# Attention, soft mixture of experts and a feed-forward layer: V's shifted copy made by GpSimd, larger expert transfers, first tokens loaded for two pairs

## The chip, the cores and the metric

The kernel runs on one core of a Trainium2 chip. The metric is device microseconds per execution; the kernel before took 448.73 us (median of three runs, 447.17 to 449.23). One further execution was profiled; it took 445.32 us, and the profile covers 443.6 us of it. Five engines matter: TensorE (PE), VectorE (DVE), ScalarE (ACT), GpSimd (POOL) and SyncE (SP), whose queue issues nearly all DMAs.

## What is computed

```python
# q, k, v: (4 batches, 8 heads, 576 tokens, 64), float32
scores = q @ k.T / 8 + slope[h] * -(i - j)      # only 0 <= i - j < 128, else -1e9
attn_out = softmax(scores) @ v                  # then (2304, 512)
logits = x @ phi                                # 32 slots: 8 experts x 4
slot_input = softmax(logits, over tokens).T @ x
slot_out[e] = relu(slot_input[e] @ w1[e]) @ w2[e]     # w1 (8,512,1024), w2 (8,1024,512)
x = softmax(logits, over slots) @ slot_out
out = leaky_relu(x @ w_in, 0.01) @ w_out        # w_in (512,2048), w_out (2048,512), float64
```

The expert weights are 33.5 MB, `w_in` and `w_out` 16.8 MB, and q, k and v 14.2 MB together.

## The kernel before

The program has three stages. The attention stage handles the 32 (batch, head) combinations as 16 pairs of heads. While it runs, the expert weights are loaded beside it into every free piece of SBUF. The expert stage then multiplies the 32 slots by the weights (`L772`, `L824`), and the feed-forward stage does the rest (`L925`, `L948`).

**A pair's work.** `load_qk` brings the tokens 64 to 575 of k and of q (256 KB each, `put` at `L185`) and the tokens 0 to 63 (32 KB each, `L186`). `relay` (RK, RQ) lets GpSimd reorder k and q in SBUF (`L255`), `turn` (TK, TQ) and `turn_rest` (TR) transpose them on PE (`L262`, `L268`), and `evac_k`, `evac_q`, `evac_rest` (EK, EQ, ER) copy the results out of PSUM. `scores` (SX, SY) multiplies (`L297`), `smax` (M) adds the mask and takes the maximum on DVE (`L314`), `expo` (E) takes the exponential on ACT (`L325`), `flip` (F) transposes (`L336`) and `flip_c` (C) copies back. `attend` (AV, `L368`) multiplies by V, `sums` and `norm` (NS, NO) divide, `turn_x` (TX, `L398`) transposes the result for the logits.

**V in two layouts.** The windows of 128 keys start at multiples of 64. `E` (`ve`) holds V with token 128 t + p on partition p, `O` (`vo`) the same shifted by 64 tokens. Both have two buffers. `load_v` loads `E` with one transfer for each head, and the last 64 tokens of `O` with a third. The other parts of `O` are copied from `E` between the two halves of the partitions by two transfers within SBUF (`L194`, `L195`):

```python
put(O[64:128, 0:4], E[0:64, 0:4], n + DVO, ("v", i))     # 130 KB
put(O[0:64, 1:4], E[64:128, 0:3], n + DVO, ("v", i))     # 97.5 KB
```

**What sets the order.** Each step of pair i stands at 2 i + `XO[step]` on one axis; the steps of the batches use `YO`. All steps are sorted by this number, and each engine gets its instructions in that order. `put` notes a transfer with its place on the axis; `issue`, called at three points in every unit, has SP issue the transfers whose place has passed (`send`, `L156`), and then as many weight pieces of 256 KB (`L171`) as a credit of `L0` (later `L1`) per unit allows. A pair takes two units of the axis. SP works through its queue strictly in order: a transfer that must wait for a buffer or for data holds back all behind it. The program also gives the DMAs eight completion counters in turn, and a DMA on one of them is issued after the DMA eight places earlier has landed.

**Weight pieces.** 71 pieces of 256 KB fit beside the attention (14 slots of 4 pieces, `qx`, `ex`, `frx`, `ql`). 26 more go into buffers that the last pairs leave, among them `nat` (6 pieces), where k and q arrive. The last 31 pieces follow in transfers of 1 MB (`L789`) as the expert stage empties the slots.

Of the kernel before, what the change touches and what calls it, by code (L numbers as in the profile page):

```python
# [18 lines left out]
def attn_softmoe_ffn(ctx: ExitStack, tc: tile.TileContext, q, k, v, phi, w1, w2, w_in, w_out, cst_in, out):  # L19
    nc = tc.nc  # L20
    B, H, S, D = q.shape
    NT, DM = out.shape
    NS = phi.shape[1]
# [11 lines left out]
    NQ, NL = 3, 8  # L35
    HI = 3
    WN = [5, 2, 0, 2, 3, 0, 0]
    XO = {"RK": -5.833, "RQ": -4.884, "TR": -4.438, "TK": -4.435, "EK": -4.019, "ER": -3.744, "TQ": -3.472, "EQ": -3.389,
# [4 lines left out]
    YO = {"lg": 4.307, "lga": 4.375, "lh": 8.258, "lgc": 8.43, "lx": 8.469, "pm": 9.118, "ln": 9.618, "bm": 9.798,  # L43
          "bmv": 10.183, "bmx": 10.399, "lnc": 10.502, "bt": 10.836, "btv": 10.874, "dxv": 10.922, "tm2": 11.205,
          "dxa": 11.366, "sl": 11.714, "bta": 11.761, "slv": 11.994, "tm3": 12.06, "tme": 12.179, "cb": 12.909,
          "cb2": 12.964, "cb3": 13.232, "ds": 13.281, "dsv": 13.416, "cb4": 14.733}
    LAST = {"li": 6.35, "lgi": 6.568}
    ZA = {"DQK": 0.8, "DV": 0.3, "DVS": 0.3, "DVO": 1.4, "W0": -2.2, "EARLY": 0.8, "L0": 2.85, "L1": 3.6, "I1": 0.7769, "I2": 0.7995, "I3": 0.86}
    DQK, DV, DVS, DVO, W0, EARLY = [ZA[x] for x in ("DQK", "DV", "DVS", "DVO", "W0", "EARLY")]
    XI = [ZA[x] % 1 for x in ("I1", "I2", "I3")]  # L50
    NEG = -1.0e30
    SLOT = 2048
# [55 lines left out]
    def put_w(i, j0, t):  # L108
        n = t.shape[1] // 512
        for j in range(n):  # L110
            W[units_w[i]][j0 + j] = t[:, 512 * j:512 * j + 512]
        return t.rearrange("p (e f) -> p e f", e=n), src_w(i, j0, j0 + n)

    with tc.manual_schedule():
# [43 lines left out]
        def put(o, i, n, key):  # L158
            bulk.insert(sum(x[2] <= n for x in bulk), (o, i, n, key))
# [17 lines left out]
        natx = [view("nat", 512, 2048 + 512 * half) for half in range(2)]  # L177

        def natr(i):
            return view("nat", 128, 3072 + 128 * (i % 2))  # L180

        def load_qk(half, i, n=-9):
            b, h = divmod(2 * i, H)
            src, t = (k, q)[half][b, h:h + 2], nat(half, i)
            put(t.rearrange("p (h c) -> p h c", h=2), src[:, 64:S, :].rearrange("h (p t) d -> p h (t d)", t=4), n, (half, i))  # L185
# [11 lines left out]
        for half in (1, 0):  # L197
            load_qk(half, 0)
        for j in range(2):
            o, i, _, _ = bulk.pop(2 - j)  # L200
# [20 lines left out]
        for half in (1, 0):  # L221
# [4 lines left out]
        load_v(1)  # L226
        issue(1)
# [7 lines left out]
        pieces += [(NG - 2 + max(XO[nm] for nm in ("TK", "TQ", "TR")) + .001, view("nat", 512, 512 * j)) for j in range(6)]  # L235

        def queue(r, t, at=None):
            i, j = divmod(nxt_piece[0] if at is None else at, 4)
            nxt_piece[0] += at is None
            low.append((r, *put_w(i, j, t)))  # L240
        nxt_piece = [0]
        late = len(pieces) + (off["x0"] - off["x2"]) // 512 + 13
        for r, t in pieces[:-6]:
            queue(r, t)
        for j in range(NL):
            queue(W0, ql[:, 512 * j:512 * j + 512], late + j)
# [126 lines left out]

# [33 lines left out]
        def batch_parts(b):  # L407
# [160 lines left out]
            def dsv():  # L568
# [3 lines left out]
                else:  # L572
# [509 lines left out]
```

## Time and profile before

| | |
|---|---|
| median of three runs | 448.73 us |
| profiled execution, its span | 445.32 us, 443.6 us |
| PE / DVE / ACT / POOL busy | 406.3 / 241.5 / 221.8 / 40.2 us |
| attention: first to last `attend` | 22.47 to 170.00 us |
| expert stage: first `L772` | 181.42 us |
| HBM read / written | 64.75 MB / 4.72 MB |

Times count from the start of the span. A busy PE is not a PE at its peak; in the attention stage the granted clock of TensorE changes from stretch to stretch, and an `attend` of 68 matmuls takes 1.99 us or up to 3.4 us. An engine's idle time is put down to what ended it. SP's rows (SPq) are the times that its queue spent on issuing.

### The profile page before, as it was taken

What the parts mean: (1) busy time and instruction counts of PE and PEld (TensorE: products, weight loads), DVE (VectorE), ACT (ScalarE), POOL (GpSimd) and SP (SyncE); (2) the same over time, 40 slices, a digit from 0 to 9 for tenths busy, and PEclk for the clock granted to TensorE, in tenths of its full rate; (3) what the DMA queues carried; (4) which work ended last, traced back from release to release, by engine and by line L of the source; (5) the groups of instructions that cost most, each with busy time, mean ns of one, the idle gap of its engine ahead of it and who ended that gap; (6) DMA issues with size and microseconds to landing.
All of it is one profiled execution on the core that took longest, in us unless ns stands there. A gap on an engine that the chain in (4) does not pass through costs nothing.

```text
span 443.6 us, 10375 instructions
## 1 busy us (share of the span) xinstructions
PE 406.3 (92%) x4012; PEld 326.6 (74%) x4012; DVE 241.5 (54%) x824; ACT 221.8 (50%) x546; POOL 40.2 (9%) x71
## 2 busy tenths in 40 slices
PE   6997779786778995999999999999999999999996
PEld 6896668586767884433777788878878888888885
DVE  2675648375658584303599867686572223225242
ACT  2765637364647471111696765555555335333330
POOL 3111111111111101202000002020202000000000
PEclk9998969898989899999999999999999999999999
DMA  5697888897998769999996203100000003003011
GB/s 154 155 290 225 256 243 235 245 264 224 258 254 253 217 159 332 350 388 392 407 396 243 95 1 118 73 0 1 1 0 1 0 0 143 1 0 144 0 72 71
DMA packets 63137, 73.88 MB, mean 167 GB/s; under 512 B 27760, under 2 KB 37360, under 8 KB 63088
## 3 DMA queue, kind: packets, MB, share of 16 engines
q1 hardware_dynamic: 62528, 72.79, 51.9%
q8 instruction: 32, 0.52, 0.5%
q10 hardware_dynamic: 560, 0.43, 0.3%
q14 instruction: 17, 0.14, 0.1%
HBM read 64.75 MB, written 4.72 MB: 157 GB/s over the span
## 4 chain that ended last, share of the span: by engine, by line
PE 75%; DMA 17%; SPq 2%; DVE 2%; issue 1%; POOL 0%; ACT 0%; ACTq 0%; DVEq 0%; POOLq 0%
PE acc L948 45%; DMA ar<-ar 8%; PE g L368 7%; DMA ar<-in_v_dram 6%; PE ph L925 4%; PE pb L772 3%; PE pb L824 3%; PE g L336 2%; PE g L262 2%; PE g L297 2%; DVE ss L314 1%; SPq L171 1%; DMA p<-in_moe_w_dram 1%; PE g L150 1%; SPq L156 1%
## 5 line engine op out<-in xcount | busy, mean ns | idle before, releaser
L948 PE MATMUL acc<-p,p 128*128 128x512 f32 x648 | 158.8, 390 | 0.0
L948 PEld LDWEIGHTS acc<-p,p 128*128 128x128 f32 x648 | 120.7, 188 | 24.6 <-issue 1.7
L938 DVE TENSOR_TENSOR p<-ar,p 128x384 fp32r<-128x384 f32 x96 | 53.0, 555 | 92.1 <-ACT ar L934 91.9
L930 ACT ACTIVATE p<-ph 128x384 fp32r<-128x384 f32 (+1 forms) x97 | 47.5, 491 | 93.1 <-PE ph L925 93.1
L368 PE MATMUL g<-ar,pt 64*64 64x65 f32 (+1 forms) x1088 | 40.1, 253 | 26.4 <-DMA ar<-ar 22.4
L368 PEld LDWEIGHTS g<-ar,pt 64*64 64x64 f32 (+1 forms) x1088 | 36.2, 162 | 30.9 <-issue 15.2
L325 ACT ACTIVATE ss<-ss,mx 128x192 f32<-128x192 f32 x144 | 51.5, 431 | 14.3 <-DVE mx L314 14.3
L948 PE MATMUL acc<-b,p 128*128 128x512 f32 x216 | 54.4, 395 | 0.0
L934 ACT ACTIVATE ar<-ph 128x384 f32<-128x384 f32 x96 | 47.0, 489 | 0.0
L948 PEld LDWEIGHTS acc<-b,p 128*128 128x128 f32 x216 | 40.1, 188 | 8.8 <-issue 0.2
L314 DVE CUSTOM_DVE_ANT_0 ss<-g,ar 128x192 f32<-128x192 f32 x128 | 38.2, 354 | 11.4 <-PE g L303 6.4
L925 PE MATMUL ph<-p,p 128*128 128x384 f32 x96 | 33.0, 349 | 0.0
L255 POOL COPY ar<-ar 128x512 f32<-128x512 f32 x32 | 19.6, 616 | 125.8 <-DMA ar<-in_k_dram 84.5
L297 PE MATMUL g<-kqt 64*64 64x192 f32 (+2 forms) x768 | 27.5, 281 | 0.0
L378 DVE TENSOR_SCALAR rs<-g 128x4 f32<-128x4 f32 x32 | 3.7, 157 | 42.5 <-PE g L368 42.5
L297 PEld LDWEIGHTS g<-kqt 64*64 64x64 f32 x768 | 24.5, 135 | 3.1 <-issue 1.8
L277 ACT ACTIVATE kqt<-g,qsc 128x512 f32<-128x512 f32 x16 | 11.0, 688 | 29.9 <-PE g L262 29.7
L336 PE MATMUL g<-ident,ss 128*128 128x128 f32 x208 | 25.9, 275 | 0.0
L718 DVE SCALAR_TENSOR_TENSOR ar<-ar 128x512 int32<-128x512 int32 x40 | 25.6, 684 | 0.2
L336 PEld LDWEIGHTS g<-ident,ss 128*128 128x128 f32 x208 | 23.8, 144 | 0.2 <-issue 0.2
L718 POOL TENSOR_TENSOR p<-ar,p 128x512 fp32r<-128x512 f32 x8 | 10.8, 1348 | 125.6 <-ACT p L718 109.0
L262 PE MATMUL g<-ident,ar 128*128 128x128 f32 x128 | 21.9, 298 | 0.0
(191 smaller groups left out, 458.4 us busy)
## 6 DMA issues: line engine op xcount, KB each, us to landing
p<-in_moe_w_dram SPq DMA_DIRECT2D x56, 256.0 KB, 4.2
p<-in_moe_w_dram SPq DMA_DIRECT2D x7, 1024.0 KB, 11.4
p<-in_moe_w_in_dram SPq DMA_DIRECT2D x5, 1024.0 KB, 9.0
p<-in_moe_w_out_dram SPq DMA_DIRECT2D x5, 1024.0 KB, 14.1
out_dram<-ar SPq DMA_DIRECT2D x17, 256.0 KB, 2.1
ar<-in_q_dram SPq DMA_DIRECT2D x16, 256.0 KB, 4.6
ar<-in_v_dram SPq DMA_DIRECT2D x32, 128.0 KB, 3.9
ar<-in_moe_w_dram SPq DMA_DIRECT2D x16, 256.0 KB, 5.3
```

The costliest lines, as they stand in the source:

```text
L262: nc.tensor.transpose(p[:, bass.ds(t, 128, step=4)], natx[half][:, 128 * t:128 * t + 128], ident)
L297: nc.tensor.matmul(sts[i, a, c][64 * u:64 * u + 64, o:o + n], lhsT=Q[r, 64 * e:64 * e + 64], rhs=K[r, 64 * e - 64 + k:64 * e - 64 + k + n] ...
L314: nc.vector.tensor_tensor_reduce(out=e[:, w], in0=p[:, w], in1=maskt[:, m:m + 192], op0=ALU.add, op1=ALU.min, accum_out=mx[i % 2][:, n:n + ...
L325: nc.scalar.activation(out=e[:, w], in_=e[:, w], func=AF.Exp, scale=-1.0, bias=mx[i % 2][:, n:n + 1])
L336: nc.tensor.transpose(p[:, 128 * j:128 * j + 128], x, ident)
L368: nc.tensor.matmul(o[n][64 * u:64 * u + 64, W * x:W * x + W], lhsT=P, rhs=V, start=bool(st), stop=bool(sp), tile_position=(r, 64 * u))
L718: l.append(lambda: f(*a, **kw))
L925: nc.tensor.matmul(p, lhsT=mst[:, 128 * f:128 * f + 128], rhs=rhs, start=True, stop=True)
L930: nc.scalar.activation(out=G[t0, f][0][:, c], in_=H1[t0, f][:, c], func=AF.Prelu, alpha=0.01)
L934: nc.scalar.activation(out=gg, in_=H1.pop((t0, f)), func=AF.Prelu, alpha=0.01)
L938: nc.vector.tensor_tensor(out=g2, in0=G0.pop((t0, f)), in1=g1.bitcast(F32), op=ALU.subtract)
L948: nc.tensor.matmul(acc[t0][t], lhsT=(g1, g1, g2)[k][:, 128 * t:128 * t + 128], rhs=(WO1, WO2, WO1)[k][c][:, i], start=(f == f0 and k == 0) ...
```

## The change

`load_v` no longer issues the two transfers within SBUF. A new step VS (`shift_v`) makes the same two copies with GpSimd instructions; it stands at 2 i - 2.49, ahead of AV at 2 i - 1.213. The 14 slots and later pieces are cut so that a slot is loaded by two transfers of 512 KB where four of 256 KB were used; a transfer of 512 KB takes two credits. The tokens 0 to 63 of k and q are loaded by `load_r` for two pairs at a time (64 KB each), so `nat` grows by 256 columns and `ex` shrinks by as many: 70 pieces fit beside the attention, and `nat` later takes 7. The numbers of `XO`, `YO`, `LAST` and `ZA` are new throughout; the transfers of k and q are now placed after both relays of the pair, the weights begin at -5.5 instead of -2.2, and `L0` is 2.55 instead of 2.85.

```diff
-    XO = {"RK": -5.833, "RQ": -4.884, "TR": -4.438, "TK": -4.435, "EK": -4.019, "ER": -3.744, "TQ": -3.472, "EQ": -3.389,
+    XO = {"RQ": -6.287, "TR": -5.772, "RK": -5.368, "ER": -5.24, "TQ": -4.686, "TK": -4.445, "EK": -4.038, "EQ": -3.861,
...
-    ZA = {"DQK": 0.8, "DV": 0.3, "DVS": 0.3, "DVO": 1.4, "W0": -2.2, "EARLY": 0.8, "L0": 2.85, "L1": 3.6, "I1": 0.7769, "I2": 0.7995, "I3": 0.86}
+    ZA = {"DQK": 0.05, "DV": 0.3, "DVS": 0.3, "W0": -5.5, "EARLY": 0.8, "L0": 2.55, "L1": 3.6, "I1": 0.7769, "I2": 0.7995, "I3": 0.86}
...
-                r, o, i = low.pop(0)
+                r, w, o, i = low.pop(0)
                 nc.sync.dma_start(out=o, in_=i)
-                credit[0] -= 1
+                credit[0] -= w
...
-            return view("nat", 128, 3072 + 128 * (i % 2))
+            return view("nat", 128, 3072 + 128 * (i % 4))
...
-            put(natr(i)[64 * half:64 * half + 64].rearrange("p (h d) -> p h d", h=2), src[:, 0:64, :].rearrange("h p d -> p h d"), n, (2, i))
+        def load_r(half, i, n=-9):
+            b, h = divmod(2 * i, H)
+            put(view("nat", 256, 3072 + 128 * (i % 4))[64 * half:64 * half + 64].rearrange("p (h d) -> p h d", h=4), (k, q)[half][b, h:h + 4, 0:64, :].rearrange("h p d -> p h d"), n, (2, i))
...
-            E, O = [w[i % NVB].rearrange("p t h d -> p t (h d)") for w in (ve, vo)]
-            put(O[64:128, 0:4], E[0:64, 0:4], n + DVO, ("v", i))
-            put(O[0:64, 1:4], E[64:128, 0:3], n + DVO, ("v", i))
...
-            pieces += [(W0, t[:, 512 * j:512 * j + 512]) for j in range(4)]
+            pieces += [(W0, t[:, 1024 * j:1024 * j + 1024]) for j in range(2)]
...
-                    load_qk(half, i + 2, 2 * i + XO["TR"] + DQK)
+                    load_qk(half, i + 2, 2 * i + max(XO[nm] for nm in ("TR", "RK", "RQ")) + DQK)
+                if i % 2 and i + 3 < NI:
+                    load_r(half, i + 3, 2 * i + XO["TR"] + DQK)
...
+        def shift_v(i):
+            flush(("v", i))
+            E, O = [w[i % NVB].rearrange("p t h d -> p t (h d)") for w in (ve, vo)]
+            nc.gpsimd.tensor_copy(O[64:128, 0:4], E[0:64, 0:4])
+            nc.gpsimd.tensor_copy(O[0:64, 1:4], E[64:128, 0:3])
```

SP's queue in a round of the middle of the attention, before: k, q and V of a later pair (`L156`), weight pieces (`L171`), the two transfers within SBUF (`ar<-ar`), and more pieces.

```order
L156 DMA ar<-in_k_dram 128x2x256
L156 DMA ar<-in_k_dram 64x2x64
L156 DMA ar<-in_q_dram 128x2x256
L156 DMA ar<-in_q_dram 64x2x64
L156 DMA ar<-in_v_dram 128x4x64 x2
L156 DMA ar<-in_v_dram 64x2x64
L171 DMA p_157<-in_moe_w_dram 128x512 x2
L171 DMA p_158<-in_moe_w_dram 128x512
L156 DMA ar<-ar 64x520
L156 DMA ar<-ar 64x390
L171 DMA p_158<-in_moe_w_dram 128x512 x3
```

Two rounds of the same part now, with the first tokens (64x4x64) in one of the two:

```order
L156 DMA ar<-in_k_dram 64x4x64
L156 DMA ar<-in_q_dram 64x4x64
L156 DMA ar<-in_k_dram 128x2x256
L156 DMA ar<-in_q_dram 128x2x256
L171 DMA p_154<-in_moe_w_dram 128x2x512
L156 DMA ar<-in_v_dram 128x4x64 x2
L156 DMA ar<-in_v_dram 64x2x64
L171 DMA p_155<-in_moe_w_dram 128x2x512
L156 DMA ar<-in_k_dram 128x2x256
L156 DMA ar<-in_q_dram 128x2x256
L171 DMA p_155<-in_moe_w_dram 128x2x512
```

A round had 15 transfers, 6 of them weight pieces. Now three transfers of V and one weight transfer follow the last row shown, and two rounds have 17 transfers: 2 of first tokens, 4 of k and q, 6 of V, and 5 of weights (10 pieces).

GpSimd's queue before, from its first relay on (`L255`; `L448` belongs to the logits):

```order
L255 COPY ar<-ar 128x512 x15
L448 TENSOR_TENSOR ar<-bm_102,ar 128x64
L255 COPY ar<-ar 128x512 x8
L448 TENSOR_TENSOR ar<-bm_102,ar 128x64
L255 COPY ar<-ar 128x512 x8
```

And now (the relay is `L257`, the copies of V are `L378` and `L379`):

```order
L257 COPY ar<-ar 128x512 x4
L378 COPY ar<-ar 64x520
L379 COPY ar<-ar 64x390
L257 COPY ar<-ar 128x512 x2
L378 COPY ar<-ar 64x520
L379 COPY ar<-ar 64x390
L257 COPY ar<-ar 128x512 x2
```

Each pair of relays now has the two copies of V of an earlier pair ahead of it, and those wait for that V to land.

PE's order around an `attend` also changed. Before, the transposes of k and q stood at its two sides and the flips (`L336`) followed in one block:

```order
L303 MATMUL g<-kqt 64x64 x2
L297 MATMUL g<-kqt 64x192 x4
L297 MATMUL g<-kqt 64x128 x4
L297 MATMUL g<-kqt 64x64 x4
L268 MATMUL g<-ident,ar 128x128
L262 MATMUL g<-ident,ar 128x128 x4
L368 MATMUL g<-ar,pt_93 64x65 x2
```

Now `attend` (`L371`) follows the scores (`L301`) at once, and the transposes (`L264`) come between the flips (`L340`) behind it:

```order
L301 MATMUL g<-kqt 64x192 x4
L301 MATMUL g<-kqt 64x128 x4
L301 MATMUL g<-kqt 64x64 x4
L371 MATMUL g<-ar,pt_93 64x65 x2
L371 MATMUL g<-ar,pt_95 64x65 x2
```

## Rows read from the trace of the kernel before

**Rows 1.** Stretches: PE, PEld, DVE, ACT, POOL busy; PE clock; DMA share; GB/s.
```profile
0.00:22.40 22.40, 18.47 (x194) 16.86 (x194) 10.19 (x58) 10.60 (x29) 4.80 (x14) 1.00 0.62 155
22.40:170.00 147.60, 120.52 (x2352) 107.66 (x2351) 93.10 (x480) 84.48 (x231) 17.26 (x30) 0.92 0.85 241
170.00:181.40 11.40, 9.18 (x142) 6.93 (x142) 5.59 (x24) 2.00 (x10) 4.17 (x11) 1.00 1.03 369
181.40:216.50 35.10, 34.83 (x313) 12.83 (x314) 8.26 (x33) 6.86 (x16) 3.22 (x8) 1.00 1.02 378
```

**Rows 2.** Chain that ended last, in order of time: start, us, what.
```profile
94.88 4.92 DMA ar<-in_v_dram
99.85 3.35 DMA ar<-ar
103.33 3.40 PE g L368 x68
```

**Rows 3.** Waits from 22.4 to 170 us: total us, times, longest (PE, then SP).
```profile
PE g L368 <- DMA ar<-ar: 19.1, 8, 3.3
...
SPq L156 <- DMA ar<-in_v_dram: 12.6, 11, 1.7
```

**Rows 4.** Timeline of SP's queue, one round: start, us, instructions.
```profile
81.83 1.13 SPq L156 DMA_DIRECT2D ar<-in_k_dram  x2
83.05 1.25 SPq L156 DMA_DIRECT2D ar<-in_q_dram  x2
84.39 1.75 SPq L156 DMA_DIRECT2D ar<-in_v_dram  x3
86.20 1.86 SPq L171 DMA_DIRECT2D p<-in_moe_w_dram  x3
88.83 1.15 SPq L156 DMA_DIRECT2D ar<-ar  x2
90.01 1.56 SPq L171 DMA_DIRECT2D p<-in_moe_w_dram  x3
...
91.67 1.14 SPq L156 DMA_DIRECT2D ar<-in_k_dram  x2
```

**Rows 5.** SP's issues of 1 MB: count, ns min/median/max, first and last start.
```profile
L789 SPq DMA_DIRECT2D p<-in_moe_w_dram x8: 367/438/4072, 182.5 to 195.5; - x8
```

**Rows 6.** Five rounds, scores to scores (columns as rows 1); first and sum.
```profile
26.94:33.71 6.77, 6.77 (x149) 6.21 (x148) 5.80 (x31) 5.65 (x16) 0.60 (x2) 1.00 0.96 285
...
sum 36.47, PE 35.16 PEld 32.31 DVE 31.23 ACT 27.97 POOL 0.87; mean PE 7.03 PEld 6.46 DVE 6.25 ACT 5.59 POOL 0.17
```

**Rows 7.** DMA issues: operation, count, KB each, median us to landing.
```profile
p<-in_moe_w_dram SPq DMA_DIRECT2D x56, 256.0 KB, 4.2
p<-in_moe_w_dram SPq DMA_DIRECT2D x7, 1024.0 KB, 11.4
...
ar<-in_v_dram SPq DMA_DIRECT2D x32, 128.0 KB, 3.9
...
ar<-ar SPq DMA_DIRECT2D x16, 130.0 KB, 3.2
```

**Rows 8.** One stretch of 10 us with DMA nearly full (columns as rows 1).
```profile
110.00:120.00 10.00, 7.40 (x152) 6.82 (x152) 6.48 (x36) 5.79 (x17) 1.08 (x2) 1.00 0.92 268
```

**Rows 9.** GpSimd's instructions on the arena: count, ns min/median/max, span, form.
```profile
L255 POOL COPY ar<-ar x32: 611/616/619, 4.9 to 150.2; 128x512 f32<-128x512 f32 x32
L718 POOL TENSOR_TENSOR p<-ar,p x8: 1307/1314/1590, 273.6 to 337.7; 128x512 fp32r<-128x512 f32 x8
```

**Rows 10.** PE's timeline at the first and last `attend`: start, us, instructions, idle before.
```profile
20.10 0.71 PE L150 MATMUL g<-ident 128*128 128x128 f32 x4
...
22.47 0.75 PE L368 MATMUL g<-ar,pt 128*64 128x65 f32 x18
...
170.00 1.99 PE L368 MATMUL g<-ar,pt 128*64 128x65 f32 x68 [3.25 <-DMA ar<-ar]
...
181.42 2.78 PE L772 MATMUL pb<-p,ar 128*32 128x512 f32 x24 [0.36 <-ACT ar L620]
```

More of the change, by code (lines that the diff above doesn't have):

```diff
@@ L37, in attn_softmoe_ffn @@
     WN = [5, 2, 0, 2, 3, 0, 0]
-    XO = {"RK": -5.833, "RQ": -4.884, "TR": -4.438, "TK": -4.435, "EK": -4.019, "ER": -3.744, "TQ": -3.472, "EQ": -3.389,
[4 rows of a table removed]
[L43 to L47, printed above, removed]
-    ZA = {"DQK": 0.8, "DV": 0.3, "DVS": 0.3, "DVO": 1.4, "W0": -2.2, "EARLY": 0.8, "L0": 2.85, "L1": 3.6, "I1": 0.7769, "I2": 0.7995, "I3": 0.86}
-    DQK, DV, DVS, DVO, W0, EARLY = [ZA[x] for x in ("DQK", "DV", "DVS", "DVO", "W0", "EARLY")]
+    XO = {"RQ": -6.287, "TR": -5.772, "RK": -5.368, "ER": -5.24, "TQ": -4.686, "TK": -4.445, "EK": -4.038, "EQ": -3.861,
[4 rows of a table added]
+    YO = {"lg": 3.21, "lga": 3.902, "lh": 6.995, "lgc": 7.809, "lx": 8.264, "pm": 8.326, "ln": 8.841, "bm": 9.098,
+          "lnc": 9.721, "bmv": 9.864, "tm2": 10.117, "bmx": 10.288, "dxv": 10.428, "tm3": 10.497, "bt": 10.674,
+          "btv": 10.881, "dxa": 10.989, "sl": 11.047, "tme": 11.471, "bta": 11.518, "slv": 11.756, "ds": 11.96,
+          "dsv": 12.03, "cb": 12.432, "cb2": 12.523, "cb3": 12.626, "cb4": 13.203}
+    LAST = {"li": 5.561, "lgi": 5.608}
+    ZA = {"DQK": 0.05, "DV": 0.3, "DVS": 0.3, "W0": -5.5, "EARLY": 0.8, "L0": 2.55, "L1": 3.6, "I1": 0.7769, "I2": 0.7995, "I3": 0.86}
+    DQK, DV, DVS, W0, EARLY = [ZA[x] for x in ("DQK", "DV", "DVS", "W0", "EARLY")]
     XI = [ZA[x] % 1 for x in ("I1", "I2", "I3")]
@@ L72, in attn_softmoe_ffn @@
     XG = 5 * 4 * D
-    sizes = [("nat", 3328), ("ex", 8512 - 3328 - XG - NVB * VW), ("x2", XG), ("vt0", VW), ("vt1", VW), ("x0", XG), ("x1", XG),
+    sizes = [("nat", 3584), ("ex", 8512 - 3584 - XG - NVB * VW), ("x2", XG), ("vt0", VW), ("vt1", VW), ("x0", XG), ("x1", XG),
              ("maskt", 384), ("xT", 1152), ("L", 336)]
@@ L179, in natr @@
         def natr(i):
-            return view("nat", 128, 3072 + 128 * (i % 2))
+            return view("nat", 128, 3072 + 128 * (i % 4))
         def load_qk(half, i, n=-9):
             b, h = divmod(2 * i, H)
-            src, t = (k, q)[half][b, h:h + 2], nat(half, i)
-            put(t.rearrange("p (h c) -> p h c", h=2), src[:, 64:S, :].rearrange("h (p t) d -> p h (t d)", t=4), n, (half, i))
-            put(natr(i)[64 * half:64 * half + 64].rearrange("p (h d) -> p h d", h=2), src[:, 0:64, :].rearrange("h p d -> p h d"), n, (2, i))
+            put(nat(half, i).rearrange("p (h c) -> p h c", h=2), (k, q)[half][b, h:h + 2, 64:S, :].rearrange("h (p t) d -> p h (t d)", t=4), n, (half, i))
+        def load_r(half, i, n=-9):
+            b, h = divmod(2 * i, H)
+            put(view("nat", 256, 3072 + 128 * (i % 4))[64 * half:64 * half + 64].rearrange("p (h d) -> p h d", h=4), (k, q)[half][b, h:h + 4, 0:64, :].rearrange("h p d -> p h d"), n, (2, i))
         def load_v(i, n=-9):
@@ L192, in load_v @@
             put(vo[i % NVB][64:128, 4, :, 0:D], v[b, h:h + VH, 512:S, :].rearrange("h p d -> p h d"), n + DVS, ("v", i))
-            E, O = [w[i % NVB].rearrange("p t h d -> p t (h d)") for w in (ve, vo)]
-            put(O[64:128, 0:4], E[0:64, 0:4], n + DVO, ("v", i))
-            put(O[0:64, 1:4], E[64:128, 0:3], n + DVO, ("v", i))
-        for half in (1, 0):
-            load_qk(half, 0)
+        for f in (load_qk, load_r):
+            for half in range(2):
+                f(half, 0)
         for j in range(2):
-            o, i, _, _ = bulk.pop(2 - j)
+            o, i, _, _ = bulk.pop(0)
             nc.scalar.dma_start(out=o, in_=i)
@@ L220, in attn_softmoe_ffn @@
         nc.vector.memset(ones, 1.0)
-        for half in (1, 0):
+        for half in range(2):
             load_qk(half, 1)
@@ L226, in attn_softmoe_ffn @@
         load_v(1)
+        for half in range(2):
+            load_r(half, 2)
         issue(1)
@@ L234, in attn_softmoe_ffn @@
         pieces += [(W0, frx)]
-        pieces += [(NG - 2 + max(XO[nm] for nm in ("TK", "TQ", "TR")) + .001, view("nat", 512, 512 * j)) for j in range(6)]
+        pieces += [(NG - 2 + max(XO[nm] for nm in ("TK", "TQ", "TR")) + .001, view("nat", 512, 512 * j)) for j in range(7)]
         def queue(r, t, at=None):
             i, j = divmod(nxt_piece[0] if at is None else at, 4)
-            nxt_piece[0] += at is None
-            low.append((r, *put_w(i, j, t)))
+            nxt_piece[0] += t.shape[1] // 512 if at is None else 0
+            low.append((r, t.shape[1] // 512, *put_w(i, j, t)))
         nxt_piece = [0]
-        late = len(pieces) + (off["x0"] - off["x2"]) // 512 + 13
-        for r, t in pieces[:-6]:
+        late = sum(t.shape[1] // 512 for _, t in pieces) + (off["x0"] - off["x2"]) // 512 + 13
+        for r, t in pieces[:-7]:
             queue(r, t)
@@ L246, in attn_softmoe_ffn @@
             queue(W0, ql[:, 512 * j:512 * j + 512], late + j)
-        for r, t in pieces[-6:]:
+        for r, t in pieces[-7:]:
             queue(r, t)
@@ L265, in turn_rest @@
         def turn_rest(i):
-            flush((2, i))
+            flush((2, i - i % 2))
             tps[2, i] = p = gt((128, 128))
@@ L347, in attend @@
         def attend(i):
-            flush(("v", i))
             E, O = ve[i % NVB], vo[i % NVB]
@@ L579, in attn_softmoe_ffn @@
         UNITS = {"TK": turn(0), "TQ": turn(1), "TR": turn_rest, "EK": evac_k, "EQ": evac_q, "ER": evac_rest, "SX": scores(0), "SY": scores(1),
-                 "RK": relay(0), "RQ": relay(1), "AV": attend,
+                 "RK": relay(0), "RQ": relay(1), "VS": shift_v, "AV": attend,
                  "NS": sums, "NO": norm, "TX": turn_x, "XT": evac_x, "XR": evac_xr}
@@ L648, in attn_softmoe_ffn @@
             for x in XI:
-                ev.append((n + x, len(ev), lambda n=n, x=x: issue(n + x, (0 if n < -3 else 1 if n < 0 else L0 / 3 if n < 26 else L1 / 3))))
+                ev.append((n + x, len(ev), lambda n=n, x=x: issue(n + x, (0 if n < -5 else L0 / 3 if n < 26 else L1 / 3))))
         for _, _, f in sorted(ev, key=lambda e: e[:2]):
```

8 rows, old and new, of the table XO are left out of this document.

## The prediction

> **What bounds the kernel now.** I read the stretches first [rows 1]. From the first `attend` to the last the attention takes 147.6 us with PE busy for 120.5 of them, at a mean granted clock of 0.92; no other engine is busier, and DMA stands at a share of 0.85. Behind it, from 170.0 to 216.5 us, PE is busy nearly throughout and DMA is full. So the attention is the stage with room, and the change touches little else.
>
> Then the chain that ended last [rows 2]: within the attention it runs again and again through a load of V, the transfer within SBUF that shifts it (`ar<-ar`), and the `attend` behind it. The waits agree [rows 3]: PE stood 19.1 us in front of `attend` until an `ar<-ar` had landed. That names the last link, not yet the bound. SP's queue does [rows 4]: one round of issues, from one load of k to the next, takes 91.67 - 81.83 = 9.84 us, and 8.70 us of it are six rows of issues that follow each other with hardly a gap; the rest is mostly the stop ahead of `ar<-ar`, where SP waits for V to land (12.6 us in 11 waits [rows 3]) and holds back everything behind it. Fifteen `attend`s after the first come in 170.00 - 22.47 = 147.5 us [rows 10], 9.84 us each as well. **SP's queue sets the pace of the attention.** The shift is only where its lateness shows: SP cannot issue the copy before V has landed, nor the next loads before the copy.
>
> What a round costs when PE isn't kept waiting stands in five rounds, measured from scores to scores [rows 6]: 36.47 us for five, 7.3 us each, with PE busy for 7.03 us at full clock, DVE for 6.25 and ACT for 5.59.
>
> **SP's part.** Before, a round's nine transfers of k, q, V and the shift took 1.13 + 1.25 + 1.75 + 1.15 = 5.28 us of SP, 0.59 us each, and its six weight pieces 1.86 + 1.56 = 3.42 us, 0.57 us each [rows 4]. Now a round has 8.5 transfers: six of k, q and V (6 x 0.59 = 3.5 us) and 2.5 of weights. A transfer of 512 KB doesn't occur before; the nearest are a piece of 256 KB, 0.57 us, and one of 1 MB, whose issue took 0.44 us in the median [rows 5]. Size does not show in it, so I take 2.5 x 0.57 = 1.4 us. Sum 4.9 us instead of 9.84, and no wait for V is left in the queue. SP stops being the bound. What is late next is DMA or PE.
>
> **DMA's part.** Per round k, q and V are 2 x 3 x 576 x 64 x 4 bytes = 0.885 MB. The order shows 5 pieces in a round, 1.31 MB; the shift's 130 KB [rows 7] and 97.5 KB, 0.233 MB, go. Together 2.20 MB. In a full stretch DMA moved 268 GB/s at a share of 0.92 [rows 8], in the first of the five free rounds 285 GB/s at 0.96 [rows 6]. That gives 8.2 or 7.7 us a round. Larger transfers may do better than either; they also land later: 256 KB took 4.2 us and 1 MB 11.4 us [rows 7], so 512 KB lies between, about 6 us. V and k/q have most of two rounds to land (two buffers each), so I count the later landing at nothing; if it isn't covered, a round grows towards the 9.84 us of now. I take 8.2 us, the row with the commoner state of the queue, for the 12 rounds in which weights are loaded at this rate, and 7.3 us, PE's own pace, for the last 3, when the 70 pieces are nearly in.
>
> **GpSimd's part.** Two copies a pair, 520 and 390 columns on 64 partitions. The relay copies 512 columns in 616 ns, within 611 to 619 in all 32 [rows 9]; by columns the new ones cost 0.63 and 0.47 us, 1.1 us a pair. No row shows a copy between partition halves. From below it can't be much less, since the columns are the same; from above the nearest row is the two-input operation of 1.31 us on 512 columns, 2.4 us a pair. With the relays (1.23 us) that is 2.3 to 3.6 us in a round of 8.2, so it is hidden either way; I take 1.1 us. The wait that is added: the copies wait on POOL for V to land, and the relays of later pairs are queued behind, with PE's transposes after them. V is issued right behind the `attend` that frees its buffer and lands in 3.9 us [rows 7], while its copy stands about 1.7 units, 7 us, further on the axis. About 3 us remain.
>
> **First and last.** Before the first `attend` PE now has no transposes of pair 2: it can start when the fillers end at 20.81 us instead of 22.47 [rows 10], a gain of 1.7 us. The weights begin earlier, which may cost the first loads up to 0.52 MB / 268 GB/s = 1.9 us each time one stands ahead; DMA's share is 0.62 there [rows 1], so nothing, with 2 us in the range. The last `attend` to the expert stage, 11.4 us [rows 10], stays. One piece of 256 KB moves behind the attention (71 to 70, `nat` 6 to 7): 0.7 us of DMA at 369 GB/s [rows 1], hidden because PE sets the pace of the expert stage. The first tokens' longer hold on `nat` costs nothing: their load is due more than two rounds ahead of its use.
>
> **Sum.** Last `attend` at 20.8 + 12 x 8.2 + 3 x 7.3 = 141.1 us instead of 170.0: 28.9 us. The profiled execution would go from 445.3 to 416.4 us. The median of the runs lies 3.4 us above it, so 419.8, say 420 us. As a check, DMA's busy time up to 216.5 us: 0.85 x 147.6 + 1.03 x 11.4 + 1.02 x 35.1 = 173 us from 22.4 us on [rows 1]. The shift's 3.64 MB at 268 GB/s take 13.6 of it, which leaves 159 us of work for the 167 us between 20.8 and 187.6. It fits, with little to spare, and loads of `w_in` and `w_out` at the end of that stretch may slip.
>
> **The rivals.**
>
> *Only the bytes count.* If the transfers were the bound already and SP's back-to-back issues merely its shadow, removing issues would be worth nothing and the gain would be the shift's 13.6 us: 435 us. For it speaks DMA's share of 0.92 and 0.96 in full stretches [rows 6, 8]; against it that the same DMA gave 285 GB/s in a round of 6.77 us, and that its share over the attention is 0.85 [rows 1]. The Trainium skill leans this way ("DMA: Bandwidth & Descriptors", "Issuing engines are not separate DMA queues"): the time an issuing sequencer needs is usually small beside the DMA itself. By that rule fewer issues buy nothing and the time is this rival's; the trace here disagrees, with 15 issues filling 8.70 of 9.84 us [rows 4].
>
> *PE alone is the bound.* If DMA delivers 285 GB/s and more, every round takes 7.3 us: 20.8 + 15 x 7.3 = 130.3, a gain of 39.7 us, 409 us. For it, the free rounds; against it, DMA's arithmetic in the check above, which such a pace would break unless loads slip.
>
> *The gain is given back.* With the attention ending earlier, more loads meet in the expert stage, where DMA is full already. Each MB pushed there costs 1/0.378 = 2.6 us once PE has to wait for weights; 4 MB would leave 420 + 10 = 430 us. Against it: PE is busy 34.83 of 35.10 us there [rows 1].
>
> *Slower: GpSimd's queue.* If a copy between halves is far slower than one in place, POOL's round, 1.23 us and two copies, becomes the pace. It passes the present 9.84 us at 4.3 us a copy; at 5 us a round takes 11.2 us, the last `attend` comes at 20.8 + 15 x 11.2 = 189 us, and the time is 445.3 + 19 + 3.4 = 468 us. For it: no row of such a copy, and every relay is queued behind. Against it: the price is seven times the relay's. The Trainium skill gives it a reason ("GPSIMD Engine Reference", "Architecture"): each of the engine's cores owns 16 partitions for ordinary compute. No run here shows what reading one half and writing the other costs.
>
> **How the numbers follow.** The forecast, 413 to 428 us, has 0.58. PE alone 0.14, only the bytes 0.12, given back 0.09, no change worth seeing 0.02, GpSimd's queue 0.05. What this kernel's measurement can tell from no change is about 0.5%, 2.2 us. Faster is the sum of the first four, 0.93; same 0.02; slower 0.05. The range goes from 408 (PE alone) to 437 (only the bytes, and 2 us of the first loads); it leaves out GpSimd's queue, no change, and some of the ends.
>
> **What the profile of the changed kernel would show.** SP's queue has no `ar<-ar` and stands idle for some 3 us a round. POOL has 32 copies at 0.63 and 0.47 us. PE's waits in front of `attend` nearly vanish, and its granted clock in the attention comes closer to 1. `attend`s are 8.2 us apart at a DMA share over 0.9, the last at about 141 us, and the first expert matmul at about 152.5 us. The prediction fails if `attend` waits on POOL for longer than on DMA before, if rounds stay above 9 us at a DMA share below 0.9, or if PE waits for weights in the expert stage.

## The result and the profile after

The changed kernel took 410.32 us in the median of four runs (410.05 to 412.08), the kernel before beside it 448.56 us (447.17 to 449.23). The ratio is 0.916, with a 95% interval of 0.913 to 0.919. The forecast was 420 us with a range of 408 to 437: the direction and the range held, and the gain is 38 us where 29 were forecast. The profiled execution took 410.25 us, its span 408.5 us.

The stretches of the kernel after: us, PE, PEld, DVE, ACT and POOL busy, PE's granted clock, DMA's share, GB/s. The first holds twelve rounds, the second the attention from the first `attend` to the last, the third the first part of the expert stage.

```profile
20.80:114.08 93.28, 89.38 (x1914) 81.79 (x1913) 75.93 (x390) 70.12 (x190) 27.46 (x48) 0.98 0.97 289
21.00:134.60 113.60, 109.70 (x2355) 100.22 (x2354) 94.39 (x488) 86.46 (x234) 32.61 (x58) 0.98 0.91 271
144.00:180.00 36.00, 35.22 (x317) 13.27 (x317) 8.49 (x37) 6.79 (x17) 4.84 (x12) 1.00 1.00 369
```

The attention has shrunk from 147.6 us [rows 1] to 113.6 us. PE was busy for 120.52 us of it before and is now for 109.70, at a mean granted clock of 0.98 instead of 0.92, and idle for 4 us instead of 27. Of the 34.0 us that went, 23.2 are PE's idle time and 10.8 its busy time, with as many matmuls (2352 and 2355) at the higher mean clock. That is a change of what bounds the stage: DMA moves 271 GB/s where it moved 241, but PE has hardly a gap left. The expert stage is as it was.

PE's timeline at the first and the last `attend` (line 371 now) and at the first expert matmul (start, us, what, count, idle before):

```profile
21.04 1.99 PE L371 MATMUL g<-ar,pt 128*64 128x65 f32 x68
...
134.63 1.99 PE L371 MATMUL g<-ar,pt 128*64 128x65 f32 x68
...
146.05 1.49 PE L781 MATMUL pb<-p,ar 128*32 128x512 f32 x12 [0.36 <-ACT ar L629]
```

These answer to [rows 10]: the last `attend` comes at 134.63 us instead of 170.00, and 11.4 us lie between it and the expert matmul, as before. No `attend` waits for V any more. The list of waits has one row left for PE in the attention (what, for what: us, times, longest), where it had 19.1 us for `ar<-ar` [rows 3]:

```profile
PE g L371 <- issue: 3.8, 2, 2.9
```

SP's queue over two rounds, from one k load to its like (start, us, what):

```profile
59.89 0.55 SPq L156 DMA_DIRECT2D ar<-in_k_dram  x1
...
61.93 2.45 SPq L156 DMA_DIRECT2D ar<-in_v_dram  x3
...
66.09 0.48 SPq L171 DMA_DIRECT2D p<-in_moe_w_dram  x1
69.20 1.65 SPq L156 DMA_DIRECT2D ar<-in_v_dram  x3
70.90 1.10 SPq L171 DMA_DIRECT2D p<-in_moe_w_dram  x2
74.62 0.61 SPq L156 DMA_DIRECT2D ar<-in_k_dram  x1
...
76.64 0.55 SPq L156 DMA_DIRECT2D ar<-in_k_dram  x1
```

With the rows left out these are 17 transfers up to 76.64 us, and their rows fill 10.60 us of 16.75: 5.3 us a round, 0.62 us each, short waits inside a row included. The queue stands 2.6 us ahead of the V load of 69.20 and as long ahead of the k load of 74.62. Against [rows 4] the queue has lost `ar<-ar` and the stop ahead of it. What it waits for now is PE, for V's buffer above all (21 to 134.6 us):

```profile
SPq L156 <- PE g L371: 16.4, 7, 5.6
```

GpSimd's instructions on the arena (count, ns min/median/max, first and last start, form):

```profile
L257 POOL COPY ar<-ar x32: 609/611/617, 4.5 to 118.3; 128x512 f32<-128x512 f32 x32
L378 POOL COPY ar<-ar x16: 612/618/626, 9.8 to 131.0; 64x520 f32<-64x520 f32 x16
L379 POOL COPY ar<-ar x16: 511/511/516, 10.5 to 131.6; 64x390 f32<-64x390 f32 x16
```

The relay costs what it did [rows 9]; the copies of V take 1.13 us a pair. POOL waits 47.5 us for V ahead of them, and nobody waits for POOL.

### The profile page after: what moved, and what is told of

It reads as the page before. It is cut to its first block, busy times and chain, and to the rows that moved or that the text cites. A ratio compares the mean times of both kernels' runs of the same rounds, so it can differ in the third digit from the quotient of the medians.

```text
span 408.5 us, 10310 instructions
## 1 busy us (share of the span) xinstructions
PE 394.6 (97%) x4008; PEld 318.2 (78%) x4008; DVE 242.3 (59%) x824; ACT 223.0 (55%) x546; POOL 58.0 (14%) x103
## 4 chain that ended last, share of the span: by engine, by line
PE 95%; issue 1%; DMA 1%; DVE 1%; ACT 0%; ACTq 0%; DVEq 0%
PE acc L957 49%; PE g L371 8%; PE g L301 6%; PE g L340 6%; PE ph L934 4%; PE g L264 4%; PE pb L781 3%; PE pb L833 3%; PE g L407 2%; PE g L150 2%; PE g L434 1%; DMA ar<-in_k_dram 1%; PE g L556 1%; PE ph L884 1%; PE ph L893 1%
## 5 line engine op out<-in xcount | busy, mean ns | idle before, releaser
L371 PE MATMUL g<-ar,pt 64*64 64x65 f32 (+1 forms) x1088 | 33.0, 225 | 3.8 <-issue 3.8
L371 PEld LDWEIGHTS g<-ar,pt 64*64 64x64 f32 (+1 forms) x1088 | 29.2, 136 | 6.7 <-issue 4.3
L340 PE MATMUL g<-ident,ss 128*128 128x128 f32 x208 | 28.8, 275 | 0.0
L727 POOL TENSOR_TENSOR p<-ar,p 128x512 fp32r<-128x512 f32 x8 | 10.8, 1349 | 125.6 <-ACT p L727 109.0
L301 PE MATMUL g<-kqt 64*64 64x192 f32 (+2 forms) x768 | 27.5, 281 | 0.0
L301 PEld LDWEIGHTS g<-kqt 64*64 64x64 f32 x768 | 24.5, 135 | 3.6 <-ACT pt L346 1.4
L340 PEld LDWEIGHTS g<-ident,ss 128*128 128x128 f32 x208 | 24.1, 144 | 0.2 <-issue 0.2
L257 POOL COPY ar<-ar 128x512 f32<-128x512 f32 x32 | 19.4, 612 | 31.0 <-issue 15.2
L934 PEld LDWEIGHTS ph<-p,p 128*128 128x128 f32 x96 | 17.9, 188 | 5.2 <-issue 1.1
L264 PE MATMUL g<-ident,ar 128*128 128x128 f32 x128 | 21.2, 291 | 0.1
L346 DVE COPY pt<-g 128x384 f32<-128x384 f32 x32 | 17.6, 549 | 4.8 <-PE g L340 4.7
```

The lines of the kernel that those rows point to most:

```text
L264: nc.tensor.transpose(p[:, bass.ds(t, 128, step=4)], natx[half][:, 128 * t:128 * t + 128], ident)
L301: nc.tensor.matmul(sts[i, a, c][64 * u:64 * u + 64, o:o + n], lhsT=Q[r, 64 * e:64 * e + 64], rhs=K[r, 64 * e - 64 + k:64 * e - 64 + k + n] ...
L340: nc.tensor.transpose(p[:, 128 * j:128 * j + 128], x, ident)
L727: l.append(lambda: f(*a, **kw))
L934: nc.tensor.matmul(p, lhsT=mst[:, 128 * f:128 * f + 128], rhs=rhs, start=True, stop=True)
```

## The experiments

Each kernel ran beside the kernel before, whose median was 447 to 449 us each time; the ratios are to it. First the parts one by one, then what the shift by transfers costs, then what bounds the kernel now.

### Which part brings the gain

**The shift alone.** `b_poolshift` is the kernel before, its order of work kept, with VS put in at 2 i - 1.2:

```diff
+          ... "CX1": -1.104, "VS": -1.2, "AV": 0.067, ...
-            put(O[64:128, 0:4], E[0:64, 0:4], n + DVO, ("v", i))
-            put(O[0:64, 1:4], E[64:128, 0:3], n + DVO, ("v", i))
+            nc.gpsimd.tensor_copy(O[64:128, 0:4], E[0:64, 0:4])
+            nc.gpsimd.tensor_copy(O[0:64, 1:4], E[64:128, 0:3])
```

> The kernel before with only the shift moved to GpSimd (placed at 2 i - 1.2); pieces of 256 KB, first tokens pair by pair and the order of before. SP's queue as the bound: the round loses 1.15 us of issues and the waits for V and comes to 7.6 us by SP; DMA's 2.46 MB at 285 GB/s need 8.6 us, so 15 x 1.2 = 18 us are gained: 430 us (415 us if DMA keeps up). Bytes alone: 13.6 us, 435 us. If the order of the tables made most of the gain: over 438 us.

It took 419.76 us, ratio 0.936 (0.929 to 0.942): three quarters of the 38 us. From the first `attend` at 20.94 us to the last at 144.68 a round takes 8.25 us. Two rounds of SP's queue, from one V load to the next but one (columns as above), have hardly a gap between their rows:

```profile
61.65 3.48 SPq L156 DMA_DIRECT2D ar<-in_v_dram  x3
65.18 2.96 SPq L171 DMA_DIRECT2D p<-in_moe_w_dram  x6
...
80.21 0.55 SPq L156 DMA_DIRECT2D ar<-in_v_dram  x1
```

With the rows left out they fill 17.65 of 18.56 us, with 13 issues a round. But a row runs from the start of its first issue to the end of its last, and SP also waits inside rows: its waits from 61.6 to 80.2 us come to 4.4 us in all, most of that for weights to land whose completion counter comes up again (what, for what: us, times, longest):

```profile
SPq L156 <- DMA p<-in_moe_w_dram: 2.6, 5, 1.0
```

So these rows alone don't show that the issues set the pace; `b_parts` below bears on it.

**The size of the weight transfers.** `a_256k` is the changed kernel with four pieces to a slot again:

```diff
-            pieces += [(W0, t[:, 1024 * j:1024 * j + 1024]) for j in range(2)]
+            pieces += [(W0, t[:, 512 * j:512 * j + 512]) for j in range(4)]
```

> The changed kernel with its slots loaded in pieces of 256 KB again; the rest as changed. If SP's queue has room now, 2.5 more issues a round (2.5 x 0.57 = 1.4 us on top of about 4.9 us, in a round of 7.6 us) cost nothing: 410 to 413 us. If the larger transfers are what raised DMA's rate above the 268 GB/s of the forecast, rounds fall back to 8.2 us and the time to about 416 us.

408.99 us, ratio 0.911 (0.906 to 0.917). The transfers of 512 KB bring nothing here. DMA moved 272 GB/s from 20 to 130 us in this kernel and 269 in the changed one. The Trainium skill ("DMA: Bandwidth & Descriptors", "Measured (HBM→SBUF, 128 partitions, SWDGE, issued from GpSimd)") advises transfers of at least 1 MB for three quarters of the peak. In its table larger transfers move more; for pieces of 256 and 512 KB, issued from SP beside loads of k, q and V, these runs don't show it.

**That and the first tokens.** `a_shiftonly` takes both of the smaller parts back and keeps the new order:

```diff
+            for j in range(i, i + 2):
+                b, h = divmod(2 * j, H)
+                put(natr(j)[...].rearrange("p (h d) -> p h d", h=2), (k, q)[half][b, h:h + 2, 0:64, :]..., n, (2, i))
...
+            pieces += [(W0, t[:, 512 * j:512 * j + 512]) for j in range(4)]
```

> The changed kernel with two of its three parts undone: weights in pieces of 256 KB and the first tokens pair by pair, so that GpSimd's copies and the new order of work are left. If those two parts are worth nothing also together: 408-412 us. If SP's issues bind the kernel again once there are 15 less the shift of them a round: 415-420 us.

417.37 us, ratio 0.935 (0.925 to 0.946), as the second reading had it: 8 us more than with the pieces alone. A round has 12 transfers instead of 11, and SP's queue is nearly full again. From one V load to the next, 11.08 us, its rows have one gap of more than 0.2 us (0.77, ahead of a load of q), and its waits come to 2.5 us in all, those inside rows included:

```profile
60.22 2.13 SPq L156 DMA_DIRECT2D ar<-in_v_dram  x3
62.40 1.53 SPq L171 DMA_DIRECT2D p<-in_moe_w_dram  x3
...
70.25 0.96 SPq L171 DMA_DIRECT2D p<-in_moe_w_dram  x2
71.30 1.59 SPq L156 DMA_DIRECT2D ar<-in_v_dram  x3
```

V comes late, so its copy does, and PE waits for POOL (what, for what: us, times, longest):

```profile
PE g L375 <- POOL ar L382: 9.3, 7, 2.7
```

That the issues make V late fits these rows and isn't shown by them alone. Whether the first tokens pair by pair would cost as much beside pieces of 512 KB was not run.

**All parts in the old order.** `b_parts` has all three edits, but the tables `XO`, `YO`, `LAST` and `ZA` of before (VS at -1.2) and the old places of the loads of k and q.

> All three parts of the change (copies by GpSimd, 512 KB weights, first tokens of two pairs at once) in the order of work of the kernel before: its tables of places, its last steps and its lead times stay. The shift alone gave 419.8 us, the whole change 410.3. If the other 9.5 us come from SP's fewer issues and the weights: 410-413 us. If they come from the new order (loads of q and k and weights issued earlier, copies put earlier): 417-421 us.

419.86 us, ratio 0.937 (0.931 to 0.943): the second reading. In the old order the two smaller parts add nothing to the shift; the last 9.5 us of the change need the new order as well.

It also answers `b_poolshift`. With 9 transfers a round in place of 13 (18 in the two rounds from 56.02 to 73.54 us) a round takes 8.22 us, from the first `attend` at 21.44 us to the last at 144.70, as long as there. SP now waits for PE to free V's buffers (20 to 145 us):

```profile
SPq L156 <- PE g L371: 26.1, 11, 6.1
```

Taking four issues a round out of the queue gave nothing. So the time of the issues is not what holds the old order at 8.2 us, or not alone; what does was not run.

### What the shift by transfers costs

**Shift by transfers in the changed kernel.** `a_dmashift` undoes only the copies by GpSimd:

```diff
+            put(O[64:128, 0:4], E[0:64, 0:4], n + 1.4, ("v", i))
+            put(O[0:64, 1:4], E[64:128, 0:3], n + 1.4, ("v", i))
...
-            nc.gpsimd.tensor_copy(O[64:128, 0:4], E[0:64, 0:4])
-            nc.gpsimd.tensor_copy(O[0:64, 1:4], E[64:128, 0:3])
```

> The changed kernel with V's shifted copy made by the two transfers within SBUF on SP's queue again, issued one unit behind V's load; no GpSimd copies. SP's queue as the old bound: SP gets back 1.15 us of issues and about 1 us of waiting for V a round, 4.9 + 2.2 = 7.1 us of 7.6, so it is nearly the bound: 412 to 418 us. Bytes as the bound: 0.233 MB a round at 285 GB/s are 0.8 us in each of 15 rounds: 422 us.

444.95 us, ratio 0.993 (0.989 to 0.997). Both expectations missed by over 20 us. With 10.5 transfers a round in place of 15 SP ought to have been free of its limit; yet the kernel is as slow as before. Its waits from 20 to 170 us, SP's first, then PE's:

```profile
SPq L156 <- DMA ar<-in_v_dram: 39.2, 14, 5.4
```

```profile
PE g L375 <- DMA ar<-ar: 26.0, 9, 5.0
```

SP stood 12.6 us in these stops before [rows 3] and stands 39.2 us now. The issues that were taken out of the queue have come back as waiting, at the same place: SP reaches the shift earlier and V lands no earlier. So in this order the pace was not set by the time that the issues take.

**The same transfers from GpSimd's queue.** `b_poolqueue` is the kernel before with the two `ar<-ar` issued by `nc.gpsimd` instead of `nc.sync`, so that SP never stops for V.

> The kernel before with the same two shift transfers, issued by GpSimd's queue instead of SP's: the same bytes, but SP neither issues them nor waits for V. SP's queue as the bound: SP's round falls to 7.6 us and DMA's 2.69 MB at 285 GB/s (9.4 us) become the bound: 15 x 0.4 = 6 us gained, 442 us, and less if DMA can do more. Bytes alone as the bound: no gain, 447 to 450 us.

442.61 us, ratio 0.988 (0.981 to 0.995). That is near the 442 us of one reading. GpSimd now waits for V in SP's place. Two issues in GpSimd's queue (start, us, what, idle before):

```profile
88.06 1.03 POOL L156 DMA_DIRECT2D ar<-ar  x2 [7.72 <-DMA ar<-in_v_dram]
...
97.89 1.18 POOL L156 DMA_DIRECT2D ar<-ar  x2 [7.62 <-DMA ar<-in_v_dram]
```

These two shifts lie 9.83 us apart, without SP's stop. The mean is less: 9.16 us from `attend` to `attend`, from the first at 28.86 us, 6.4 us later than before, to the last at 166.29. DMA is full here (columns of the stretches):

```profile
60.00:100.00 40.00, 33.64 (x650) 29.93 (x649) 25.86 (x135) 22.97 (x65) 8.72 (x17) 0.91 1.02 267
```

So this run does not refute the reading by which DMA needs 9.4 us a round. A second wait could hold the pace as well. V's two buffers make one: `attend` frees a buffer, V is loaded into it, the shift follows, and only then comes the `attend` after next.

**The shift behind the next V load.** `a_dmalate` and `b_dmalate` put the transfers one pair later in SP's queue, where V has landed long ago: `n + 1.4` becomes `n + 2.4` in `a_dmashift`, and `DVO` 2.4 in the kernel before.

> The changed kernel with the shift by two transfers again, as in a_dmashift, but put into SP's queue behind the next pair's V load instead of a unit behind its own, so that V has landed by the time that SP comes to it. Theory 1 (SP's in-order stop for V's landing held back the next loads: in a_dmashift it is 39.2 us over 14 stops): the stop goes, the loads run on, and the time falls from 445 to 412-425 us. Rival (the shift's bytes, about 0.23 MB a round, or its own landing before each attend, are what costs): it stays at 438-450 us. In between (427-437) both would have a part, and PE's waits ahead of attend would show the shift's landing as the last to come.

> The kernel before with one number changed, the place of the shift in SP's queue, from 1.4 to 2.4 units, so behind the next pair's V load. Theory 1 (the in-order stop is the cost): 425-436 us, as much as the part of the 28.5 us of the GpSimd copies that bytes and landings do not take back. Rival (bytes of the shift and issues of SP, which both stay): 444-452 us. Rival (the shift lands too late for its attend and V's two buffers come free later): 450-470 us.

450.09 us, ratio 1.004 (1.000 to 1.008), and 454.49 us, ratio 1.014 (1.008 to 1.020), the latter as its third reading had it. The first theory fell in this form. In `a_dmalate` SP's largest wait is now for PE, not for V (20 to 170 us), and the queue shows why:

```profile
SPq L156 <- PE g L375: 18.1, 8, 3.4
```

```profile
80.97 1.99 PE L375 MATMUL g<-ar,pt 128*64 128x65 f32 x68
...
91.77 3.49 PE L375 MATMUL g<-ar,pt 128*64 128x65 f32 x68 [3.46 <-DMA ar<-ar]
```

```profile
82.88 2.50 SPq L156 DMA_DIRECT2D ar<-in_v_dram  x3
85.43 1.24 SPq L156 DMA_DIRECT2D ar<-ar  x2
```

The next V load waits for the `attend` of 80.97 to free its buffer; the shift that the following `attend` needs is queued behind that load, is issued at 85.43 and is awaited until 91.77. One in-order wait was traded for another.

**A third buffer for V.** `a_dma3` is `a_dmalate` with three buffers, and `a_dma3wait` the same with the shift back ahead of the next V load, so that only SP's stop for V returns:

```diff
-    VH, NVB = 2, 2
+    VH, NVB = 2, 3
...
+            put(O[64:128, 0:4], E[0:64, 0:4], n + 2.4, ("v", i))   # a_dma3wait: n + 1.4
+            put(O[0:64, 1:4], E[64:128, 0:3], n + 2.4, ("v", i))
...
+        load_v(2, XO["AV"] + DV - 2)
```

> The changed kernel with the shift by two transfers on SP's queue again, but with three buffers for V in place of two, and each shift put behind the next pair's V load, as in a_dmalate. Theory 2 (what the two transfers cost is their place in a chain of two V buffers: attend ends, V is loaded 5-7 us, the shift lands 3-7 us later, the attend after next may start; two rounds of it last about 20 us): a third buffer gives the chain a round more, nothing waits, and the time is 412-425 us, with PE's waits for the shift below 5 us in all. Rival (the shift's 0.23 MB a round on DMA engines that are busy over 0.9 of the time): 438-450 us, as a_dmashift and a_dmalate. Two early pieces of weights are loaded later for want of room, which costs nothing if the expert stage still starts 11.4 us behind the last attend.

> As a_dma3 (shift by transfers, three buffers for V), but each shift back at its place in a_dmashift, one unit behind its own V load and ahead of the next pair's, so that SP stops for V's landing again. It parts the two waits that a_dma3 took away together. If SP's in-order stop by itself sets the pace (V's landing of 5-7 us, then the issues up to the next V load, about 3 us, are one round of 9-10 us, whatever the number of buffers): 438-448 us, as a_dmashift, with SP's stops for V over 25 us in all. If the chain through two buffers alone was the cost: 424-432 us, as a_dma3.

`a_dma3` took 427.09 us, ratio 0.957 (0.947 to 0.967), 2 us over its expectation; `a_dma3wait` 446.55 us, ratio 1.001 (0.997 to 1.005). The same bytes, the same issues and the same buffers, and 19 us between them: they hang on whether SP stops for V ahead of the next loads. SP's waits from 20 to 150 us, without the stop and with it:

```profile
SPq L156 <- DMA ar<-in_v_dram: 5.9, 9, 1.5
```

```profile
SPq L156 <- DMA ar<-in_v_dram: 36.0, 14, 5.5
```

One round of `a_dma3wait` in SP's queue:

```profile
67.85 1.72 SPq L156 DMA_DIRECT2D ar<-in_v_dram  x3
69.62 1.01 SPq L171 DMA_DIRECT2D p<-in_moe_w_dram  x1
75.87 1.11 SPq L156 DMA_DIRECT2D ar<-ar  x2
...
78.20 0.47 SPq L171 DMA_DIRECT2D p<-in_moe_w_dram  x1
78.71 1.81 SPq L156 DMA_DIRECT2D ar<-in_v_dram  x3
```

V's load and landing take 8.0 us, the shift and the issues behind it 2.8 us, and then the next V load may go: 10.9 us, in series, although there are three buffers. This round is one of the longer ones; the mean is 9.70 us from `attend` to `attend` (19.52 to 165.06 us), beside 9.84 in the kernel before.

Four kernels are the four combinations of SP's stop and the number of V's buffers. With the stop they took 444.95 us with two buffers (`a_dmashift`) and 446.55 with three (`a_dma3wait`); without it 450.09 with two (`a_dmalate`) and 427.09 with three (`a_dma3`). So either the stop or the two buffers is enough to hold the pace: taking one away gave nothing, taking both gave 18 us. GpSimd's copies take the stop out of SP's queue, and in the chain through the two buffers 1.13 us stand where a transfer had to be issued and to land.

The 17 us between `a_dma3` and the changed kernel were not taken apart. The profiled execution took 431.7 us, 4.6 us above the median. PE still waits there for the shift (20 to 150 us), 11.0 us where the expectation had less than 5, and the transfers land late in a full DMA (20 to 130 us: operation, count, KB, median us to landing), 6.4 us in place of a copy of 1.13:

```profile
PE g L377 <- DMA ar<-ar: 11.0, 3, 5.5
```

```profile
q1 hardware_dynamic: 35484, 30.58, 102.6%
...
ar<-ar SPq DMA_DIRECT2D x11, 130.0 KB, 6.4
```

### What bounds the kernel now

**More bytes.** `a_extra` loads k a second time in ten rounds, 256 KB each, into a buffer that is free:

```diff
+            if half == 0 and 2 <= i < 12:
+                put(frx.rearrange("p (h c) -> p h c", h=2), k[b, h:h + 2, 64:S, :]..., n, ("x", i))
```

> The changed kernel with one more transfer of 256 KB in ten rounds (k is loaded a second time into a buffer that nobody reads), so more bytes than the removed shift had, and nothing waits for them. Theory 2 (the chain, not the bytes): 410-414 us. Rival (the DMA's bytes set the pace, 0.256 MB at 280 GB/s are 0.91 us in each of ten rounds): 417-421 us. If the bytes of the shift were the whole loss of a_dmashift: 440 us or more.

412.26 us, ratio 0.925 (0.915 to 0.934): 1.9 us more than the changed kernel by the medians, 4 us by the ratios, whose intervals overlap. More bytes a round than the shift had, in ten rounds, cost 2 to 4 us; the shift cost 34.6 (`a_dmashift`). In the window of the twelve rounds DMA moved 306 GB/s in it, where the changed kernel had 289 (columns of the stretches):

```profile
20.80:114.08 93.28, 86.25 (x1841) 77.72 (x1840) 73.51 (x379) 67.81 (x184) 26.42 (x47) 1.00 1.04 306
```

So the transfers had room, and the bytes of the shift were at most a small part of what held the kernel before.

**Weights spread wider.** `a_l0_23` is the changed kernel with `L0` 2.3 for 2.55.

> The changed kernel with the weight pieces of the attention spread wider (credit 2.3 for 2.55), so that the DMA is less full in the first rounds. If the 2.9 us stop of PE in the fifth attend comes from instructions that are fetched late while the DMA is full: that stop shrinks or goes and the time is 406-410 us. If the weights are then late for the expert stage: 412-418 us. If neither: 410 +- 1.

414.45 us, ratio 0.925 (0.920 to 0.931): 4 us slower. The time lies in the range of late weights, but the first expert matmul still follows 11.4 us behind the last `attend` (149.68 and 138.26 us), so its cause stays open. The run doesn't decide what the stop comes from, since its DMA was as full ahead of PE's stop of 2.9 us, and the stop was still there:

```profile
40.00:50.00 10.00, 8.83 (x221) 8.16 (x213) 8.30 (x48) 8.59 (x24) 2.72 (x5) 1.00 1.03 266
```

## Why the prediction was right, and where it failed

**The sum.** Five terms make up the difference between 419.8 and 410.3 us. The twelve rounds took (114.08 - 21.04) / 12 = 7.75 us instead of 8.2, which is 5.4 us less. The last three took (134.63 - 114.08) / 3 = 6.85 us instead of 7.3, another 1.4. The 3.4 us by which the median lay above the profiled execution before did not appear after (410.32 against 410.25). The first `attend` came at 21.04 us instead of 20.8, 0.2 more, and the way from the last `attend` to the end is 275.6 us instead of the 275.3 taken over. 419.8 - 5.4 - 1.4 - 3.4 + 0.2 + 0.3 = 410.1.

**The mis-sized term** is the rate of DMA. I priced a round by the row with 268 GB/s [rows 8]. In the twelve rounds DMA moved 289 GB/s at a share of 0.97, nearer the row I set aside [rows 6], and that is 2.2 to 2.3 MB in 7.75 us; `a_extra` shows that it could do more. PE bounds these rounds: 89.38 of 93.28 us busy, 7.45 us a round where the free rounds had 7.03 [rows 6]. So the rival "PE alone" had the bound right, and my argument against it, that DMA's arithmetic leaves no room, did not hold: a share near 1 was no limit on what could still be moved. That its 409 us lie so near is partly luck: it takes 7.3 us for each of 15 rounds, where the mean was 7.57, and contains the 3.4 us that did not appear. A slip beside it: sixteen shifts of 0.233 MB are 3.73 MB, not 3.64, which moves "only the bytes" by 0.3 us.

**The step that failed** is "SP's queue sets the pace of the attention", as I meant it: 15 issues that fill 8.70 of 9.84 us. I read the rest, SP's stop for V, as a remainder. `a_dmashift` has a third fewer issues and the stop grows from 12.6 to 39.2 us at the same pace; `a_dma3wait` against `a_dma3` shows that the stop alone is enough, and `a_dmalate` that two buffers without it are too. A queue that is busy nine tenths of the time looked like the bound and was partly filling time in which it would have waited. "The shift is only where its lateness shows" was wrong in the same way: the shift was the cause. What I forecast for the change still came out near, and as far as the cause goes that was luck: the copies by GpSimd remove the stop and two issues at once and shorten the chain through the buffers, and the new pace was worked out from DMA and PE, whatever had held the old one.

Whether the time of the issues binds once the shift is gone stays open. `b_poolshift` and `b_parts` take the same time with 13 and with 9 transfers a round; `a_shiftonly`, with 12, is 8 us slower than `a_256k`, with 11. The Trainium skill's rule, cited ahead of the result ("DMA: Bandwidth & Descriptors", "Issuing engines are not separate DMA queues"), is that the time to issue a transfer is usually small beside the transfer. `a_dmashift` and `b_parts`, where fewer issues bought nothing, agree with it; `a_shiftonly` speaks against it and does not decide it. The trace that I set against it, issues that fill 8.70 of 9.84 us, showed a busy queue and not a bound.

**What held.** GpSimd's copies were priced at 0.63 and 0.47 us and took 0.618 and 0.511, hidden. SP's part was put at 4.9 us a round and is 5.3, with the 3 us of idle time forecast. The larger weight transfers and the later landing (V 5.2 us instead of 3.9) cost nothing. PE's waits ahead of `attend` and `ar<-ar` are gone, the clock rose to 0.98, and the 11.4 us up to the expert stage stayed. "Only the bytes" (435 us), "given back" (430) and "GpSimd's queue" (468) did not occur.

## What to carry to other kernels

A transfer that must wait for another to land, issued in order on the queue that also issues the next loads, puts the landing into every round; see how long the queue stops there and what stands behind it before counting its issues. A buffer chain can hold the same pace a second time, so that removing either wait alone shows nothing. To learn whether a busy queue is the bound, take issues out and see whether its waits grow by as much; a row of several issues can hold waits too.

## What the runs showed of the hardware

A copy by GpSimd from one half of the partitions to the other was no dearer than one in place: 618 ns for 64 x 520 and 511 ns for 64 x 390, beside 611 ns for the relay's 128 x 512.

A shift by transfer landed 6.4 us after its issue in the profiled execution of `a_dma3` at a DMA share of 1.03. In `a_dma3wait`, at 0.85, the same transfers took 2.7 us (medians, 20 to 130 us). That the fuller DMA makes the difference is argued, not shown by a run:

```profile
q1 hardware_dynamic: 30561, 26.39, 84.9%
...
ar<-ar SPq DMA_DIRECT2D x10, 130.0 KB, 2.7
```

PE stopped for 2.9 us in the middle of an `attend` with nothing to wait for that the trace shows (PE's timeline after):

```profile
48.13 1.65 PE L371 MATMUL g<-ar,pt 128*64 128x65 f32 x50
52.65 0.88 PE L371 MATMUL g<-ar,pt 64*64 64x65 f32 x18 [2.88 <-issue]
```

DMA's queues from 41 to 50 us, then from 50 to 52.6 us (packets, MB, share): the first nine hold no packet of the queue that brings instructions, and one comes just before PE goes on.

```profile
q1 hardware_dynamic: 3078, 2.51, 102.5%
```

```profile
q1 hardware_dynamic: 1025, 0.76, 102.5%
q8 instruction: 1, 0.02, 2.6%
```

Such stops came to 3.8 us in the changed kernel. `b_parts` had a longer one (21 to 135 us):

```profile
PE g L434 <- issue: 3.7, 1, 3.7
```

That instructions come late while DMA is full is argued from these rows and not shown by a run.
